# Retention plus MLP on one core: attention rewritten from whole-row scores per head to 128-token chunks with a running state

## The chip, the cores and the metric

The kernel runs on one core of one Trainium2 chip. The metric is device time in microseconds (us). "Span" is the profiled time from the first to the last instruction, about 2 us less than the time. PE is the tensor engine, PEld its weight loads, DVE the vector engine, ACT the scalar engine, POOL the GpSimd engine, SP the queue that issues DMAs. In a profile line, `L331` is a line of the kernel's source, and names such as `ml<-xt,win` are output tile and input tiles, with buffer numbers left out.

## The reference

Eight batches, eight heads, 576 tokens, head size 64. Retention is attention without a softmax, with a decay per head; its output is a 4,608 x 512 matrix that feeds an MLP of width 2,048.

```python
scores = (1/sqrt(64)) * q @ k.T
gamma  = 1 - 2.0 ** (-5 - head)
ret    = scores * where(i >= j, gamma ** (i - j), 0)
x      = (ret @ v), heads side by side          # 4608 x 512
h      = x @ w_in                               # 512 -> 2048
out    = (h * cos(h)) @ w_out                   # 2048 -> 512
```

`gamma ** (i - j)` splits into `gamma ** i * gamma ** -j`, so the decay can be put on rows and columns. Both kernels do that.

## The kernel before

It is scheduled by hand. For each batch, q and k come in 32-column pieces, are transposed 32 x 32 by DVE, and every head computes all scores of the lower triangle. ACT evicts them with the column decay, POOL masks the diagonal blocks, and PE multiplies with v.

```python
def attn_head_m1(self, b, c, hp):            # scores of one head
    for r in range(NCH):                     # five key blocks
        segs = [(0, 512), (512, wq - 512)] if r == 0 else [(0, wq)]
        ...
            te.matmul(dst, lhsT, rhs, ...)   # K = 64, N = 512,64,448,320,192,64
        ...
            act.activation(RT, PR, AF.Copy, scale=w_ap)      # eviction
        ...
        pool.affine_select(RTM, RT, ...)     # diagonal mask
# attn_head_m2: 12 matmuls v^T x scores into po_a and po_b
# batch loop: per head, m1 of the next head, then 4 units of MLP layer 1
#   (or 1 unit of layer 2), then m2 of this head
self.boot_pending = self.make_kv_issue_list(1) + [self.prologue_w_in, self.prologue_w_out]
# moe_mlp1_unit, first unit: waits until ALL MLP weights are in
self.S_w.wait(te, self.v_wout)
```

Of the kernel before, what the change touches and what calls it, by code (L numbers as in the profile page):

```python
# [6 lines left out]
ALU = mybir.AluOpType  # L8
# [4 lines left out]
B_, H_, S_, D_ = 8, 8, 576, 64  # L13
DFF = 2048
DM = H_ * D_
CH = 128
NCH = (S_ + CH - 1) // CH
TOK = B_ * S_
TB = 512
NTB = TOK // TB  # L20
QF = 4 * S_


class _Ctr:

    def __init__(self, handle, step=1):
        self.h = handle
        self.step = step
        self.count = 0

    def mark(self, inst):
        self.count += self.step
        inst.then_inc(self.h, self.step)
        return self.count

    def wait(self, eng, val):
        if val > 0:
            eng.wait_ge(self.h, val)


class _RR:

    def __init__(self, n):
        self.n = n
        self.next = 0
        self.last_consumer = [None] * n

    def take(self):
        s = self.next
        self.next = (self.next + 1) % self.n  # L50
        prev = self.last_consumer[s]
        return s, prev

    def set_consumer(self, s, key, val):
        self.last_consumer[s] = (key, val)


def bass_retnet_parallel__then__act_gcu_kernel(
    nc: bass.Bass,
    q: bass.AP,  # L60
    k: bass.AP,
    v: bass.AP,
    moe_w_in: bass.AP,
    moe_w_out: bass.AP,
    out: bass.AP,
):
    es = contextlib.ExitStack()
    with es:
        kern = _Kernel(nc, es, q, k, v, moe_w_in, moe_w_out, out)
        kern.build()  # L70


class _Kernel:
    def __init__(self, nc, es, q, k, v, w_in, w_out, out):
        self.nc = nc
        self.es = es
        self.q = q.tensor
        self.k = k.tensor
        self.v = v.tensor
        self.w_in = w_in.tensor  # L80
        self.w_out = w_out.tensor
        self.out = out.tensor

        self.gam = [float(1.0 - 2.0 ** (-5.0 - h)) for h in range(H_)]
        self.lng = [math.log(g) for g in self.gam]

        def sb(name, shape, dt):
            return nc.alloc_sbuf_tensor(name, shape, dt)

        self.XT = [sb(f"xt{c}", [128, TOK], BF16) for c in range(4)]  # L90
        self.WIN = sb("win", [128, 4 * DFF], BF16)
        self.WOUT = sb("wout", [128, 16 * DM], BF16)
        self.INQ = [sb(f"inq{i}", [128, QF], F32) for i in range(2)]
        self.INK = [sb(f"ink{i}", [128, QF], BF16) for i in range(2)]
        self.VNF = NCH * H_ * D_
        self.TQ = sb("tq32", [128, S_], F32)
        self.QH = [sb(f"qh{i}", [128, QF], BF16) for i in range(2)]
        self.KTB = [sb(f"ktb{i}", [128, QF], BF16) for i in range(2)]
        self.NVBF = 3
        self.VBF = [sb(f"vbf{i}", [128, self.VNF], BF16) for i in range(self.NVBF)]  # L100
        self.NRT = 12
        self.RT = [sb(f"rt{i}", [128, S_], BF16) for i in range(self.NRT)]
        self.NRM = 12
        self.RTM = [sb(f"rtm{i}", [128, CH], BF16) for i in range(self.NRM)]
        self.GT = sb("gt", [128, 16 * TB], BF16)
        self.NCB = 3
        self.CB = [sb(f"cb{i}", [128, TB], BF16) for i in range(self.NCB)]
        self.NOSB = 2
        self.OSB = [sb(f"osb{i}", [128, DM], F32) for i in range(self.NOSB)]
        self.IG = sb("ig", [128, S_], F32)  # L110
        self.IP = sb("ip", [128, 1], F32)
        self.UP = [sb(f"up{c}", [128, S_], F32) for c in range(4)]
        self.WV = sb("wv", [128, H_ * NCH], F32)
        self.C_LN8 = sb("c_ln8", [128, 1], F32)
        self.C_PIH = sb("c_pih", [128, 1], F32)

        self.PO_A = [nc.alloc_psum_tensor("po_a0", [128, 512], F32)]
        self.POB = nc.alloc_psum_tensor("po_b", [128, 512], F32)
        self.NPR = 6
        self.PR = [nc.alloc_psum_tensor(f"pr{i}", [128, 512], F32) for i in range(self.NPR)]  # L120

        def sem(name, step=1):
            return _Ctr(self.es.enter_context(nc.semaphore(name)), step)

        self.S_q = [sem("s_q0", 16), sem("s_q1", 16)]
        self.S_k = [sem("s_k0", 16), sem("s_k1", 16)]
        self.S_v = [sem(f"s_v{i}", 16) for i in range(3)]
        self.S_w = sem("s_w", 16)
        self.S_out = [sem("s_out0", 16), sem("s_out1", 16)]
        self.P = {  # L130
            "dve": sem("p_dve"),
            "act": sem("p_act"),
            "pool": sem("p_pool"),
            "pe": sem("p_pe"),
        }
        self.eng = {
            "dve": nc.vector,
            "act": nc.scalar,
            "pool": nc.gpsimd,
            "pe": nc.tensor,  # L140
            "sp": nc.sync,
        }

        self.pr_rr = _RR(self.NPR)
        self.rt_rr = _RR(self.NRT)
        self.rm_rr = _RR(self.NRM)
        self.cb_rr = _RR(self.NCB)
        self.osb_rr = _RR(self.NOSB)

        self.v_wout = 0  # L150
        self.v_win = 0
        self.seq_prep_last = {}
        self.seq_vcast = {}
        self.seq_pair_kt = {}
        self.seq_xt = {}
        self.seq_m1_last = {}
        self.seq_m2_last = {}
        self.seq_gt_last = {}
        self.seq_mlp2_last = {}
        self.n_out_dma = [0, 0]  # L160
        self.out_idx = 0
        self.seq_xtb_last = None
        self.seq_xtb = {}

    @staticmethod
    def sA(tile, fsize, p0, np_, c0, ncols, cstep=1):
        return bass.AP(tile, p0 * fsize + c0, [[fsize, np_], [cstep, ncols]])

    @staticmethod
    def sA3(tile, fsize, p0, np_, c0, n1, s1, n2, s2=1):  # L170
        return bass.AP(tile, p0 * fsize + c0, [[fsize, np_], [s1, n1], [s2, n2]])

    def mark(self, key, inst):
        return self.P[key].mark(inst)

    def wait(self, key_waiter, key_target, val):
        if val is not None and val > 0:
            self.P[key_target].wait(self.eng[key_waiter], val)

    def build(self):  # L180
        nc = self.nc
        blk = self.es.enter_context(nc.Block())

        @blk.tensor
        def _(eng):
            self.emit()

    def emit(self):
        self.prologue()
        self.issue_q_dmas(0)  # L190
        self.issue_kv_dmas(0, spread=False)
        self.issue_q_dmas(1)
        self.prep_wave(0)
        self.boot_pending = self.make_kv_issue_list(1) + [self.prologue_w_in, self.prologue_w_out]
        self.head_state = {}
        self.attn_head_m1(0, 0, 0)
        n_iter = B_ + 2
        for b in range(n_iter):
            has_att = b < B_
            j = b - 1  # L200
            has_moe = 0 <= j < NTB
            u1 = list(range(16)) if has_moe else []
            u2 = list(range(4)) if has_moe else []
            if has_att:
                self.pending_kv = self.make_kv_issue_list(b + 2) if b + 2 < B_ else []
                if b + 2 < B_:
                    self.issue_q_dmas(b + 2)
                heads = [(u // 2, u % 2) for u in range(8)]
                for u in range(8):
                    c, hp = heads[u]  # L210
                    if u < 7:
                        nc_, nhp = heads[u + 1]
                        self.attn_head_m1(b, nc_, nhp)
                    elif b + 1 < B_:
                        self.attn_head_m1(b + 1, 0, 0)
                    if u < 4:
                        for _ in range(4):
                            if u1:
                                self.moe_mlp1_unit(j, u1.pop(0))
                    else:  # L220
                        if u2:
                            self.moe_mlp2_unit(j, u2.pop(0))
                    if u == 3:
                        for dt in u1:
                            self.moe_mlp1_unit(j, dt)
                    self.attn_head_m2(b, c, hp)
                    if hp == 1:
                        self.xt_eval_A(b, c)
                    if u >= 4 and b + 1 < B_:
                        self.prep_pair(b + 1, u - 4)  # L230
# [451 lines left out]
```

## Time and profile before

| | before |
|---|---|
| time, median of 3 runs | 458.96 us |
| span | 457.0 us |
| first MLP matmul | 72.97 us |
| busy PE, ACT, DVE, POOL | 86, 56, 50, 38% |

The page of the kernel before: its span, the busy share of each engine, then PE and DMA in 40 equal slices of the span (tenths busy; one slice is 11.4 us).

```profile
span 457.0 us, 7084 instructions
...
PE 391.6 (86%) x2304; PEld 191.3 (42%) x2304; DVE 228.0 (50%) x372; ACT 257.5 (56%) x578; POOL 172.7 (38%) x409
...
PE   0283476999999999999999999999999999989987
...
DMA  9999999964696469746964696450011001101102
```

There are two stages. For six slices PE has little to do while DMA is full. After that PE is full. The waits of the kernel before (engine, tile and line, what it waited for: us in total, times, longest):

```profile
PE pr L418 <- DVE ktb L386: 20.3, 1, 20.3
...
PE po_a L495 <- POOL rtm L441: 14.3, 3, 9.0
...
PE pr L575 <- DMA wout<-in_moe_w_out_dram: 7.8, 1, 7.8
PE pr L575 <- ACT rt L428: 7.0, 27, 0.3
```

The first three are the start. The PE timeline of the kernel before (start us, length us, engine, line, operation, operands, count, idle before) shows the first MLP matmuls and, later, the steady repetition:

```profile
72.97 6.42 PE L575 MATMUL pr<-xt,win 128*128 128x512 bf16 x16 [7.76 <-DMA wout<-in_moe_w_out_dram]
...
144.43 3.63 PE L618 MATMUL pr<-wout,gt 128*128 128x512 bf16 x16 [0.26 <-ACT rt L428]
147.98 0.24 PE L495 MATMUL po_a<-rtm,vbf 128*64 128x128 bf16 x1
148.06 0.33 PE L521 MATMUL po_a<-rt,vbf 128*64 128x384 bf16 x1
...
148.92 0.97 PE L418 MATMUL pr<-qh,ktb 64*128 64x512 bf16 x6
150.15 1.04 PE L618 MATMUL pr<-wout,gt 128*128 128x512 bf16 x4 [0.26 <-ACT rt L428]
```

One head takes 150.15 - 144.43 = 5.72 us: 3.55 us of MLP (16 matmuls at about 0.216 us plus a short lead-in), 0.94 us of outputs, and 1.23 us of scores and a wait. Compare start times with start times: a record of an MLP matmul is about 379 ns long while the matmuls start 216 ns apart, so neighbouring records overlap.

### The profile page before, as it was taken

Reading aid. Unit: us, or ns where it says so; the run is one execution under the profiler, and the core shown is the slowest. Engines: PE = TensorE matmul, PEld = TensorE weight load, DVE = VectorE, ACT = ScalarE, POOL = GpSimd, SP = SyncE. Lnnn points to the kernel's source line nnn. Section 1 sums busy time; section 2 is a strip of 40 time slices with the busy share of each in tenths; the row PEclk is TensorE's granted clock in tenths of the full one; section 3 lists DMA queues with packets and bytes.
Section 4 is the critical chain, followed back from the end, with each engine's and each line's share of the span. In section 5 each row is a group of like instructions: output and inputs, shape, how many; then the busy total and the mean of one; then the engine's idle time right before and its main releaser. Section 6 shows DMA issues by size and latency. Waiting matters only on the chain.

```text
span 457.0 us, 7084 instructions
## 1 busy us (share of the span) xinstructions
PE 391.6 (86%) x2304; PEld 191.3 (42%) x2304; DVE 228.0 (50%) x372; ACT 257.5 (56%) x578; POOL 172.7 (38%) x409
## 2 busy tenths in 40 slices
PE   0283476999999999999999999999999999989987
PEld 0051232444444444444444444444444444434433
DVE  0440271546754675467546754675467542471641
ACT  8563272864686458645864586458645864260630
POOL 8093980445444544454445444532233222000000
PEclk9999999999999999999999999999999999999999
DMA  9999999964696469746964696450011001101102
GB/s 117 137 126 119 169 200 152 103 26 70 90 115 29 68 90 116 29 68 89 118 27 70 85 120 27 70 77 0 1 47 47 0 1 47 47 0 49 44 14 79
DMA packets 193908, 32.97 MB, mean 72 GB/s; under 512 B 186704, under 2 KB 188752, under 8 KB 193872
## 3 DMA queue, kind: packets, MB, share of 16 engines
q0 software_dynamic: 114448, 13.64, 48.4%
q1 hardware_dynamic: 79424, 18.88, 24.4%
q8 instruction: 19, 0.31, 0.3%
q14 instruction: 17, 0.14, 0.1%
HBM read 36.70 MB, written 9.44 MB: 101 GB/s over the span
## 4 chain that ended last, share of the span: by engine, by line
PE 75%; ACT 9%; DMA 8%; issue 4%; POOL 3%; DVE 0%; ACTq 0%; POOLq 0%; DVEq 0%
PE pr L575 29%; PE pr L618 28%; ACT rt L428 9%; PE pr L418 5%; PE po_a L495 5%; PE po_a L521 4%; DMA wout<-in_moe_w_out_dram 4%; DMA vbf<-in_v_dram 3%; PE po_b L507 2%; PE po_b L535 2%; POOL ink L329 1%; POOL vbf L339 1%; POOL rtm L441 0%; DVE gt L597 0%; ACT cb L587 0%
## 5 line engine op out<-in xcount | busy, mean ns | idle before, releaser
L428 ACT ACTIVATE rt<-pr,wv 128x512 bf16<-128x512 f32 (+5 forms) x384 | 148.6, 486 | 130.9 <-PE pr L418 130.9
L441 POOL TENSOR_SCALAR_AFFINE_SELECT rtm<-rt 128x128 bf16<-128x128 bf16 (+1 forms) x320 | 97.2, 324 | 198.3 <-ACT rt L428 191.9
L575 PE MATMUL pr<-xt,win 128*128 128x512 bf16 x576 | 132.3, 385 | 15.9 <-DMA wout<-in_moe_w_out_dram 7.8
L618 PE MATMUL pr<-wout,gt 128*128 128x512 bf16 x576 | 129.5, 379 | 10.2 <-ACT rt L428 7.0
L597 DVE TENSOR_TENSOR gt<-pr,cb 128x512 bf16<-128x512 f32 x144 | 97.1, 690 | 76.7 <-ACT cb L587 73.5
L587 ACT ACTIVATE cb<-pr,c_pih 128x512 bf16<-128x512 f32 x144 | 95.9, 688 | 48.6 <-PE pr L575 44.9
L575 PEld LDWEIGHTS pr<-xt,win 128*128 128x128 bf16 x576 | 54.7, 99 | 82.2 <-issue 12.8
L418 PE MATMUL pr<-qh,ktb 64*128 64x512 bf16 (+5 forms) x384 | 68.7, 301 | 20.3 <-DVE ktb L386 20.3
L618 PEld LDWEIGHTS pr<-wout,gt 128*128 128x128 bf16 x576 | 53.9, 98 | 75.0 <-ACT rt L428 9.9
L635 DVE COPY osb<-pr 128x512 f32<-128x512 f32 x36 | 24.9, 692 | 96.6 <-PE pr L618 96.6
L495 PE MATMUL po_a<-rtm,vbf 128*64 128x128 bf16 x256 | 54.5, 237 | 15.8 <-POOL rtm L441 14.3
L418 PEld LDWEIGHTS pr<-qh,ktb 64*128 64x128 bf16 (+1 forms) x384 | 29.2, 100 | 55.5 <-DVE ktb L386 20.3
L495 PEld LDWEIGHTS po_a<-rtm,vbf 128*64 128x64 bf16 x256 | 29.7, 116 | 44.7 <-issue 23.7
L521 PE MATMUL po_a<-rt,vbf 128*64 128x384 bf16 (+2 forms) x192 | 46.6, 291 | 0.0
L535 PE MATMUL po_b<-rt,vbf 128*64 128x64 bf16 x256 | 42.1, 201 | 0.0
L339 POOL DMA_DIRECT2D vbf<-in_v_dram x40 | 34.1, 858 | 10.6 <-issue 9.2
L329 POOL DMA_DIRECT2D ink<-in_k_dram x32 | 35.9, 1126 | 4.5 <-issue 4.5
L378 DVE STREAM_TRANSPOSE tq<-inq 128x576 f32<-128x576 f32 x32 | 24.9, 778 | 19.7 <-DMA ink<-in_k_dram 18.0
L546 DVE CAST xt<-po_b 64x64 bf16<-64x64 f32 x64 | 14.0, 219 | 31.5 <-PE po_b L507 31.1
L535 PEld LDWEIGHTS po_b<-rt,vbf 128*64 128x64 bf16 x256 | 28.9, 118 | 0.0
L380 DVE TENSOR_TENSOR qh<-tq,up 128x576 bf16<-128x576 f32 x32 | 24.2, 758 | 1.1
L386 DVE STREAM_TRANSPOSE ktb<-ink 128x576 bf16<-128x576 bf16 x32 | 24.7, 770 | 0.0
(19 smaller groups left out, 88.9 us busy)
## 6 DMA issues: line engine op xcount, KB each, us to landing
inq<-in_q_dram SPq DMA_DIRECT2D x32, 288.0 KB, 6.8
out_dram<-osb SPq DMA_DIRECT2D x36, 256.0 KB, 2.0
ink<-in_k_dram POOLq DMA_DIRECT2D x32, 144.0 KB, 6.1
vbf<-in_v_dram POOLq DMA_DIRECT2D x32, 128.0 KB, 4.7
win<-in_moe_w_in_dram POOLq DMA_DIRECT2D x8, 256.0 KB, 7.5
wout<-in_moe_w_out_dram POOLq DMA_DIRECT2D x1, 2048.0 KB, 20.0
vbf<-in_v_dram POOLq DMA_DIRECT2D x8, 64.0 KB, 2.6
```

Of the source, the lines that this page charges most:

```text
L329: self.S_k[slot].mark(pool.dma_start(dst, src))
L339: self.S_v[vpar].mark(pool.dma_start(dst, src))
L418: pm = self.mark("pe", te.matmul(dst, lhsT, rhs, start=True, stop=True))
L428: av = self.mark("act", act.activation(self.sA(self.RT[rts], S_, 0, ck, co, ncols), self.sA(self.PR[slot], 512, 0, ck, 0, ncols), AF.Copy, ...
L441: msk = pool.affine_select(self.sA(self.RTM[rms], CH, 0, ck, 0, ck), self.sA(self.RT[rts], S_, 0, ck, 0, ck), pattern=[[1, ck]], compare_o ...
L495: mm = te.matmul(self.sA(self.PO_A[0], 512, 64 * hp, 64, q0, ck), vmat, self.sA(self.RTM[rms], CH, 0, ck, 0, ck), start=(seen_a == 1), sto ...
L521: mm = te.matmul(self.sA(self.PO_A[0], 512, 64 * hp, 64, q0 + ck, nA), vmat, self.sA(self.RT[rts], S_, 0, ck, ck, nA), start=(seen_a == 1) ...
L535: mm = te.matmul(self.sA(self.POB, 512, 64 * hp, 64, 0, S_ - 512), vmat, self.sA(self.RT[rts], S_, 0, ck, 512 - q0, S_ - 512), start=(seen ...
L575: mm = te.matmul(self.sA(self.PR[slot], 512, 0, 128, 0, TB), self.sA(self.WIN, 4 * DFF, 0, 128, c2 * DFF + 128 * dt, 128), self.sA(self.XT ...
L587: sin = self.mark("act", act.activation(self.sA(self.CB[cb], TB, 0, 128, 0, TB), self.sA(self.PR[slot], 512, 0, 128, 0, TB), AF.Sin, bias= ...
L597: gm = self.mark("dve", ve.tensor_tensor(self.sA(self.GT, 16 * TB, 0, 128, dt * TB, TB), self.sA(self.PR[slot], 512, 0, 128, 0, TB), self. ...
L618: mm = te.matmul(self.sA(self.PR[slot], 512, 0, 128, 0, DM), self.sA(self.GT, 16 * TB, 0, 128, c3 * TB + 128 * stt, 128), self.sA(self.WOU ...
```

## The change

The intent is to do less attention work on PE and none that grows with the square of the sequence, to load q, k and v as they lie in memory, and to start the MLP sooner. Attention now goes in 40 chunks (eight batches of 128, 128, 128, 128 and 64 tokens), all eight heads at once. A chunk has four steps:

- T: eight PE transposes of q and k into PSUM bank `tp`, one ACT copy to `qk`.
- S: eight score matmuls, one DVE multiplication with a triangle, to `pt`.
- ST: four matmuls that add this chunk's k^T v to the state in PSUM bank `st`; DVE copies it masked to `sbd`.
- O: four matmuls from the old state and eight within the chunk, both into bank `tp` again; DVE scales to `xt`.

Steps are dealt out between the MLP's pieces, each of four 128x512 matmuls. The first layer of block j+1 alternates with the second layer of block j. A small recorder derives every wait from what each operation reads and writes. The diff, cut to its core (`...` marks what is left out; the comments are added here):

```diff
-    def prep_pair(self, b, c):                # DVE 32x32 transposes of q and k
-    def attn_head_m1(self, b, c, hp): ...     # ACT evictions, POOL masks
-    def attn_head_m2(self, b, c, hp): ...
+    def load_chunk(self, g):                  # fp32, rows of 64 values = 256 bytes
+        for i in (1, 0, 2):
+            self.P.add("sp", lambda e, i=i: e.dma_start(...))
+    def cast(self, g, engs): ...              # to bf16, v times its decay
+    def step_t(self, g): ...
+    def step_s(self, g): ...
+    def step_st(self, g): ...
+    def step_o(self, g): ...
+    def bank(self):
+        i = self.n_ml % 4
+        self.n_ml += 1
+        return i, self.ML[i]
+    def mlp1(self, j, f):
+        i, ps = self.bank()
...
+    def mlp2(self, j, t, qd):
+        if qd == 0:
+            self.m2 = self.bank()
...
+        if qd == 3:
+            self.P.add("act", lambda e: e.activation(self.OS[o].ap(), ps.ap(), AF.Copy), ...)
...
+        load_to(4)
+        cast_to(4, ("act", "dve", "pool"))
+        for s in range(4):
+            self.load_win(s)
+        for s in range(4):
+            self.load_wout(s)
+        load_to(self.NSTG)
+        done = need[0]
+        for g in range(done):                 # the first four chunks, alone
+            for st in steps(g):
+                st()
+        for j in range(-1, NTB):
...
+            for i in range(16):
+                if j + 1 < NTB:
+                    self.mlp1(j + 1, i)
+                while k < n * (2 * i + 1) / 32:
+                    todo[k]()
+                    k += 1
+                if j >= 0:
+                    self.mlp2(j, i // 4, i % 4)
+                while k < n * (2 * i + 2) / 32:
+                    todo[k]()
+                    k += 1
```

PSUM is laid out in eight banks of 512 fp32 columns: `tp` 1, `sc` (scores) 2, `st` 1, `ml` (both MLP layers) 4.

## The prediction

> **What bounds the kernel now.** The tensor engine (PE), in two ways. (a) Start: in the timeline PE has only batch 0's attention before 72.97 us, when the first MLP matmul starts; the waits name the `wout` load. The page's slices show DMA full for about 90 us. (b) From 73 us on PE is over 90% busy. The chain of waits repeats every 5.72 us, once per head: 16 MLP matmuls (3.55 us), 12 output matmuls (0.94), 6 score matmuls (0.97), and 0.26 waiting for ACT's score eviction. After the last head, two MLP blocks run alone at 0.216 us per 128x512 matmul (13.97 us for 64). DVE, ACT, POOL: 50, 56, 38%.
>
> **What changes.**
> - MLP: the same 1,152 matmuls x 0.216 = 249 us, the floor.
> - Attention on PE: 1,152 matmuls streaming 204,800 columns become 1,216 streaming about 141,000, transposes included. In the timeline the output matmuls of N=128 and 64 start 0.06 and 0.03 us apart, so weight loads hide. The Trainium skill, "TensorE: Matmul & The Clock Gate", section Back-to-back issue gap, gives 81 ns sustained for N=128; this trace shows about 60, which I use: 32 x 0.06 = 1.9 us for a full chunk, 1.1 for a 64-row chunk, 1.8 on average. Before: 8 heads x 2.2 = 17.4 us per batch; after: 5 x 1.8 = 9. Saved: about 8 us for each of 7 batches in the PE-bound stage.
> - New stalls: one PSUM bank (`tp`) serves transposes and outputs; each chunk is a chain (transpose, ACT copy of 1,024, scores, DVE mask of 1,024, output, DVE scaling). Extrapolating the traced evictions (ACT 310 ns at 64 to 687 at 512 columns, DVE 690 at 512), copy and mask take 1.1 and 1.2 us. With 1 or 2 MLP pieces of 0.86 us between steps, copy and scaling are sometimes late: 0.5 us a chunk, 15 us.
> - DVE loses 64 transposes; ACT loses 149 us of score evictions, gains about 40 of copies; POOL loses 320 masks, gains 3 casts a chunk (about 2.5 us). All stay under 65%.
> - Start: loads come in 256-byte pieces, and MLP weights are asked for after four chunks (about 22 us) instead of at 48.7. Before, they took 24 us from issue. I expect the first MLP matmul near 30 us, the first MLP block with five chunks until about 57 (partly starved by the chunk chain), no later weight stall.
>
> **Sum.** 57 + remaining MLP 235 + 31 chunks x 1.8 = 55 + stalls 15 + tail 4 = 366 us span, plus 2 us between span and time: 368 us, range 350 to 400. All of it is on the critical path, since PE is it. Faster by over 2%: 0.98; within 2%: 0.015; slower: 0.005.
>
> **What would show each step.** First `win` matmul at 25 to 38 us; `wout` waits under 5 us. In the middle, one MLP block (128 matmuls) plus about 4.4 chunks takes 37 to 40 us. Attention matmuls start about 0.06 us apart. PE waits on ACT (`qk`) and DVE (`xt`) total 10 to 30 us. POOL under 40%, DVE 50 to 60%. No gap between the last block's two layers.
>
> **What would make it wrong.** Loads of 128 weight columns not hiding behind N=128 matmuls (100 ns each: +35 us). The `tp` chain stalling 1 us a chunk more (+35). 256-byte pieces still delaying `wout` past 70 us (+15). Score pairs on disjoint rows, and output pairs on disjoint columns, running together (-15).

## The result, and the profile after

| | before | after |
|---|---|---|
| time, median of 4 runs | 458.88 us | 390.91 us |
| span | 457.0 us | 389.2 us |
| first MLP matmul | 72.97 us | 38.02 us |
| from there to the end | 384.0 us | 351.2 us |
| busy PE, ACT, DVE, POOL | 86, 56, 50, 38% | 84, 42, 48, 23% |

The ratio is 0.8531 (95% interval 0.8512 to 0.8549). A ratio is the mean time of one kernel's fast runs over that of the other's of the same rounds, so it is not quite the ratio of the medians quoted.

The change is faster, inside the predicted range, but 23 us slower than the predicted 368. Of the gain, 35 us come from the earlier start of the MLP and 33 us from the time after it. The page of the changed kernel (a slice is 9.7 us here):

```profile
span 389.2 us, 5828 instructions
...
PE 326.4 (84%) x2325; PEld 160.0 (41%) x2368; DVE 185.4 (48%) x283; ACT 162.3 (42%) x231; POOL 91.3 (23%) x128
...
PE   1156877889988999989889999998999899989996
...
PEclk9999989999999999999999999999999999999999
```

PE is the engine with most to do again, but its digits are not an unbroken row of nines. `PEclk` is the granted clock in tenths; the 8 in its sixth slice comes up again below. The waits of the changed kernel that concern PE:

```profile
PE sc L247 <- ACT qk L236: 16.7, 14, 9.8
PE ml L331 <- ACT os L361: 15.3, 25, 0.9
PE tp L227 <- DVE xt L309: 6.5, 7, 2.0
...
PE ml L331 <- DVE xt L309: 3.9, 3, 1.9
...
PE ml L331 <- DVE gt L340: 3.5, 4, 1.0
```

The second line, first-layer matmuls that wait for the copy of a second-layer output, is nowhere in the prediction. The PE timeline of the changed kernel at the start:

```profile
7.31 0.60 PE L227 MATMUL tp<-idn,nat 128*128 128x128 bf16 x4 [2.15 <-ACT nat L210]
17.72 0.61 PE L247 MATMUL sc<-qk 64*128 64x128 bf16 x8 [9.80 <-ACT qk L236]
...
38.02 1.48 PE L331 MATMUL ml<-xt,win 128*128 128x512 bf16 x3 [1.20 <-DVE xt L309]
...
72.77 1.04 PE L331 MATMUL ml<-xt,win 128*128 128x512 bf16 x4 [1.88 <-DVE xt L309]
```

And ACT's timeline just before those first scores:

```profile
16.12 0.63 ACT L210 ACTIVATE nat<-stg 128x512 bf16<-128x512 f32 x1 [2.99 <-DMA stg<-in_q_dram]
16.66 1.00 ACT L236 ACTIVATE qk<-tp 128x1024 bf16<-128x1024 bf16 x1
```

Chunk 0's transposes are finished before 8 us, but ACT copies them at 16.66 us, because the casts of q for all four first chunks stand ahead of the copy in ACT's order, and the fourth has to arrive first. Then four chunks run one after another, 5.5 us each. The first MLP block (first layer of block 0 with five chunks) lasts from 38.02 to 72.77 us, 34.8 us.

In the middle, the PE timeline of the changed kernel shows what the steps cost and the new wait:

```profile
196.44 0.61 PE L227 MATMUL tp<-idn,nat 128*128 128x128 bf16 x8
196.88 1.03 PE L351 MATMUL ml<-wout,gt 128*128 128x512 bf16 x4
198.71 1.04 PE L331 MATMUL ml<-xt,win 128*128 128x512 bf16 x4 [0.80 <-ACT os L361]
199.68 0.40 PE L247 MATMUL sc<-qk 64*128 64x128 bf16 x8
200.01 1.04 PE L351 MATMUL ml<-wout,gt 128*128 128x512 bf16 x4
200.88 1.03 PE L331 MATMUL ml<-xt,win 128*128 128x512 bf16 x4
201.74 0.39 PE L267 MATMUL st<-nat 128*128 128x128 bf16 x4
201.97 1.03 PE L351 MATMUL ml<-wout,gt 128*128 128x512 bf16 x4
```

Two MLP pieces with nothing between start 0.864 us apart (200.01 to 200.88 is one). With S between they start 1.30 us apart (198.71 to 200.01), so S costs 0.44 us. ST costs 200.88 to 201.97 less 0.864, or 0.23; T and O come out in the same way at 0.45 and 0.67. A full chunk takes 1.78 us of PE, 56 ns for each of its 32 matmuls on average: what the prediction had (1.9).

From 196.88 to 198.71 is 1.83 us, though: more than a full piece is lost. The blocks in the middle take (341.19 - 72.77) / 7 = 38.3 us (341.19 us is where the last pair of layers starts).

### The profile page after: what moved, and what is told of

Same layout as the page of the kernel before. It is cut to its first block, busy times and chain, and to the rows that moved or that the text cites. A ratio compares the mean times of both kernels' runs of the same rounds, so it can differ in the third digit from the quotient of the medians.

```text
span 389.2 us, 5828 instructions
## 1 busy us (share of the span) xinstructions
PE 326.4 (84%) x2325; PEld 160.0 (41%) x2368; DVE 185.4 (48%) x283; ACT 162.3 (42%) x231; POOL 91.3 (23%) x128
## 4 chain that ended last, share of the span: by engine, by line
PE 73%; ACT 12%; DVE 7%; issue 3%; SPq 3%; DMA 1%; DVEq 0%; ACTq 0%
PE ml L331 31%; PE ml L351 30%; ACT qk L236 5%; ACT os L361 4%; PE tp L227 4%; PE sc L247 3%; ACT cb L338 3%; DVE gt L340 3%; PE tp L299 3%; SPq L185 3%; DVE pt L255 2%; DVE xt L309 2%; PE st L267 1%; DMA stg<-in_q_dram 1%; PE tp L289 1%
## 5 line engine op out<-in xcount | busy, mean ns | idle before, releaser
L340 DVE TENSOR_TENSOR gt<-ml,cb 128x512 bf16<-128x512 f32 x144 | 99.5, 691 | 160.3 <-ACT cb L338 142.1
L338 ACT ACTIVATE cb<-ml,cpi 128x512 bf16<-128x512 f32 x144 | 98.9, 687 | 168.8 <-PE ml L331 168.8
L331 PE MATMUL ml<-xt,win 128*128 128x512 bf16 x549 | 147.4, 387 | 24.9 <-ACT os L361 15.3
L351 PE MATMUL ml<-wout,gt 128*128 128x512 bf16 x560 | 143.4, 380 | 2.2 <-issue 0.9
L331 PEld LDWEIGHTS ml<-xt,win 128*128 128x128 bf16 x576 | 50.4, 99 | 84.0 <-ACT os L361 22.9
L351 PEld LDWEIGHTS ml<-wout,gt 128*128 128x128 bf16 x576 | 52.2, 98 | 57.2 <-ACT os L361 1.2
L212 POOL CAST nat<-stg 128x512 bf16<-128x512 f32 (+1 forms) x72 | 42.5, 613 | 140.6 <-PE st L267 117.1
L214 POOL TENSOR_TENSOR nat<-stg,wv 128x512 bf16<-128x512 f32 (+1 forms) x40 | 41.7, 1043 | 61.8 <-PE tp L299 38.6
L255 DVE TENSOR_TENSOR pt<-sc,tri 128x1024 bf16<-128x1024 f32 (+1 forms) x40 | 44.3, 1109 | 13.8 <-PE sc L247 13.7
L236 ACT ACTIVATE qk<-tp 128x1024 bf16<-128x1024 bf16 (+1 forms) x40 | 37.3, 933 | 24.1 <-PE tp L227 24.1
L247 PE MATMUL sc<-qk 64*128 64x128 bf16 (+1 forms) x320 | 16.4, 226 | 16.7 <-ACT qk L236 16.7
L247 PEld LDWEIGHTS sc<-qk 64*128 64x128 bf16 (+1 forms) x320 | 9.5, 102 | 33.8 <-ACT qk L236 26.1
L276 DVE TENSOR_TENSOR sbd<-st,bdm 128x512 bf16<-128x512 f32 x32 | 21.8, 681 | 0.0
L299 PE MATMUL tp<-pt,nat 128*64 128x128 bf16 (+1 forms) x320 | 16.7, 230 | 2.9 <-DVE pt L255 2.9
```

Source lines behind the costliest of these rows:

```text
L212: fn = lambda e, dst=dst, src=src: e.tensor_copy(dst, src)
L214: self.P.add(engs[2], lambda e: e.tensor_tensor(ap(nat, 3 * DM, 0, n, 2 * DM, [D, H], [1, D]), ap(stg, 3 * DM, 0, n, 2 * DM, [D, H], [1, D ...
L236: self.P.add("act", lambda e: e.activation(ap(qk, 1024, 0, 128, 0, [128, 8], [1, n]), tb.rearrange("p (c n) -> p c n", c=8)[:, :, 0:n], AF ...
L247: inst = e.matmul(ap(self.SC, 1024, 0, n, hp * 512 + c * 128, [1, n]), ap(qk, 1024, 64 * hp, 64, c * 128, [1, n]), ap(qk, 1024, 64 * hp, 6 ...
L255: self.P.add("dve", lambda e: e.tensor_tensor(ap(pt, 1024, 0, n, 0, [128, 8], [1, n]), ap(self.SC, 1024, 0, n, 0, [128, 8], [1, n]), ap(se ...
L299: inst = e.matmul(ap(self.T, 512, 64 * hp, 64, c * 128, [1, n]), ap(na, 3 * DM, 0, n, 2 * DM + (2 * c + hp) * D, [1, D]), ap(pt, 1024, 0, ...
```

## The experiments

Twelve kernels ran, all with correct results, each timed in three rounds against the kernel before. "Against the change" is (ratio - 0.8531) x 457.9 us. The 95% interval of a ratio reaches 0.6 to 1.3 us to each side (2.7 for e9_jit_bank), so a difference of under about 1.5 us between two rows is not clear of noise.

| run | what | median us | ratio | against the change |
|---|---|---|---|---|
| e1_jit | first casts in order of need | 384.74 | 0.8397 | -6.1 |
| e2_bank | MLP banks 2 + 2 | 369.10 | 0.8071 | -21.1 |
| e8_onebank | MLP banks 2 + 1 | 373.48 | 0.8164 | -16.8 |
| e3_split | banks 2 + 1, own bank for O | 366.07 | 0.7993 | -24.6 |
| e4_wlate | w_out loads later | 392.72 | 0.8565 | +1.6 |
| e5_unp | head halves not alternating | 391.77 | 0.8573 | +1.9 |
| e9_jit_bank | e1 + e2 | 366.30 | 0.7966 | -25.9, two speeds (below) |
| e6_jit_split | e1 + e3 | 364.80 | 0.7974 | -25.5 |
| e11_jit_bank_wl | e1 + e2 + e4 | 362.14 | 0.7900 | -28.9 |
| e10_all | e1 + e3 + e4 | 358.46 | 0.7827 | -32.2 |
| e12_serial | steps not interleaved | 495.95 | 1.0826 | +105 |
| e7_before_early | kernel before, weights earlier | 466.52 | 1.0195 | - |

### The late start: order on ACT (e1_jit)

```diff
-        cast_to(4, ("act", "dve", "pool"))
+        cast_to(1, first)
...
         for g in range(done):
-            for st in steps(g):
-                st()
+            self.step_t(g)
+            if g + 1 < done:
+                cast_to(g + 2, first)
+            self.step_s(g)
+            self.step_st(g)
+            self.step_o(g)
```

> The casts of the first four chunks are moved to one chunk ahead of their use, so ACT's first copy of transposes no longer stands behind the cast of the fourth chunk's q. Theory 'order on ACT' (the start is late because of the order in ACT's queue): the 9.8 us wait of the first scores shrinks to under 2 us, the first MLP matmul moves from 38.0 to 28 to 31 us, and the whole gets 5 to 9 us shorter than 390.9 (382 to 386). Rival 'loads bind the start' (bandwidth decides when the first MLP block can end): the first MLP matmul moves, but the block's end near 72.8 us does not, and the whole gains under 2 us.

The wait of the scores in this run, and its PE timeline:

```profile
PE sc L247 <- ACT qk L236: 7.6, 13, 1.1
```

```profile
29.32 1.48 PE L331 MATMUL ml<-xt,win 128*128 128x512 bf16 x3 [1.19 <-DVE xt L309]
...
64.97 1.21 PE L331 MATMUL ml<-xt,win 128*128 128x512 bf16 x4 [1.88 <-DVE xt L309]
```

The longest wait of scores fell from 9.8 to 1.1 us. The first MLP matmul came 8.7 us sooner, the end of the first block 7.8 us sooner, the whole 6.1 us sooner. The order of the casts was the cause of that part of the late start; the edit moves those on DVE and POOL too, and that ACT's order was the one that held up the scores is read from the trace (the copy at 16.66 us directly behind the cast at 16.12). The 1.7 us lost again after the first block go with the clock: between 65.7 and 69.1 us it was granted at 0.50 in this run and not in the changed kernel, and 3.4 us at half speed are worth 1.7. The one run of the four without that stretch, by its mean clock of 0.996, took 383.34 us. The rival, that bandwidth fixes the block's end, fell for this kernel.

### The wait for the output copy: PSUM rotation (e2_bank)

Four banks are handed out in turn. For each 128-token output the program takes one bank for a first-layer unit, one for the second-layer output, then three for first-layer units. The next taking is the fourth after the second-layer output's, so with four banks it gets the same bank, and it comes immediately after that output's last matmul. It must wait for ACT's copy (0.60 us) each time.

```diff
-    def bank(self):
-        i = self.n_ml % 4
+    def bank1(self, j):
+        i = self.n_ml % (4 if j == 0 else 2)
         self.n_ml += 1
         return i, self.ML[i]
+    def bank2(self):
+        self.n_m2 += 1
+        i = 2 + self.n_m2 % 2
+        return i, self.ML[i]
```

> First MLP layer gets PSUM banks 0 and 1 (all four in the block without a second layer), second layer gets 2 and 3, instead of four in one rotation. Theory 'bank collision' (every fifth taking of a bank lands on the one whose output copy has just started): the waits of first-layer matmuls on the output copy fall from 15.3 us to under 2, the middle blocks from 38.3 to about 36.5 us, the whole by 12 to 17 us to 374 to 379. Rival 'the wait only hides another' (ACT or DVE would be late anyway): under 5 us gained, with the wait turning up on gt or cb.

The only waits of first-layer matmuls (line 336 here) that the list of this run still has, and then, from its PE timeline, where the second block starts and where the last pair of layers starts:

```profile
PE ml L336 <- DVE xt L309: 5.2, 5, 1.9
...
PE ml L336 <- issue: 1.6, 9, 0.3
```

```profile
72.76 1.04 PE L336 MATMUL ml<-xt,win 128*128 128x512 bf16 x4 [1.87 <-DVE xt L309]
...
322.69 1.03 PE L336 MATMUL ml<-xt,win 128*128 128x512 bf16 x4
```

For comparison, the last pair of layers in the changed kernel, its start and one collision:

```profile
341.19 1.02 PE L331 MATMUL ml<-xt,win 128*128 128x512 bf16 x4 [0.78 <-DVE gt L340]
...
347.23 1.03 PE L351 MATMUL ml<-wout,gt 128*128 128x512 bf16 x4
348.95 1.04 PE L331 MATMUL ml<-xt,win 128*128 128x512 bf16 x4 [0.69 <-ACT os L361]
```

In e2_bank the wait on `os` is gone, and so is the one on `gt`. A middle block takes (322.69 - 72.76) / 7 = 35.7 us, 2.6 less. I expected 12 to 17 us and got 21: the idle time listed (15.3 us, 0.69 us for one wait in the undisturbed last pair of layers) starts only at the modelled end of the last matmul, while the starts there are 1.72 us apart (347.23 to 348.95) instead of 0.864, so one collision costs 0.86 us. The mean clock was the same in both runs (0.995 and 0.996). This wait is by itself nearly the difference between the measured 391 us and the predicted 368; but the agreement is partly luck, since two other terms were off in opposite directions (below).

### One bank for transposes and outputs (e3_split and e8_onebank)

```diff
+        self.TO = nc.alloc_psum_tensor("to", [128, 512], F32)
...
-        self.ML = [nc.alloc_psum_tensor(f"ml{i}", [128, 512], F32) for i in range(4)]
+        self.ML = [nc.alloc_psum_tensor(f"ml{i}", [128, 512], F32) for i in range(3)]
...
-                    ap(self.T, 512, 0, 128, c * 128, [1, n]),
+                    ap(self.TO, 512, 0, 128, c * 128, [1, n]),
...
+    def bank1(self, j):
+        i = self.n_ml % (3 if j == 0 else 2)
...
+    def bank2(self):
+        return 2, self.ML[2]
```

The lines with `TO` are in e3_split only. The second layer always has bank 2, the first layer banks 0 and 1.

> Second layer gets one bank of its own, first layer two, and the bank this frees takes the attention outputs, so that transposes and outputs no longer share one. Theory 'shared transpose bank': as with the bank split alone, plus the waits of transposes on the xt scaling (6.5 us, most of it before 73 us) and part of the starved first block go: 4 to 8 us better than the bank split alone, 367 to 373. Rival 'the single second-layer bank brings the copy wait back': no better than the bank split alone, with waits of second-layer matmuls on the output copy.

> Only the bank part of the third run: one bank for the second layer, two for the first, transposes and outputs sharing a bank as in the changed kernel (a PSUM bank stays unused). Splits the 24.8 us of that run: if the single bank costs 2 to 3 us against two, 371 to 373 us, and the separate output bank was worth about 6; if the single bank is free, 369, and the output bank was worth 3.

One bank for the second layer instead of two costs 4.3 us (0.8164 against 0.8071). The separate output bank is then worth 7.8 us (0.7993 against 0.8164). Both are more than I had estimated, and they partly cancel: e3_split is only 3.6 us better than e2_bank, just under the 4 to 8 expected, because its rival was in part right (second-layer matmuls wait 3.0 us for `os` again). The end of the first block in e3_split:

```profile
65.35 1.04 PE L335 MATMUL ml<-xt,win 128*128 128x512 bf16 x4 [1.88 <-DVE xt L310]
```

It comes at 65.35 us instead of 72.77, and no wait of transposes on `xt` is left. So the shared bank did cost what the prediction had feared of it, but in the first block and not in the middle: between 72.8 and 341 us the changed kernel's transposes wait 0.5 us for `xt` in total.

### Loads (e4_wlate, e6_jit_split, e9_jit_bank, e10_all, e11_jit_bank_wl)

```diff
-        for s in range(4):
-            self.load_wout(s)
...
             def prep():
+                if 4 <= g < 8:
+                    self.load_wout(g - 4)
```

> The four loads of the second layer's weights are asked for later, one each ahead of the transposes of chunks 4 to 7, so that input chunks 5 to 8 compete with less. Theory 'loads bind the first block': input loads after 22 us land sooner, the first block (38.0 to 72.8 us) shortens by 2 to 6 us, the whole with it. Rival 'the chunk chain binds the first block': within 1 us of 390.9, or slower if the weights now come late.

Alone it gained nothing. POOL's cast of chunk 6's v starts at 41.21 us instead of 46.23, so the loads did come sooner, but the first block still ended at 73.11 us: the chain of steps bound it (the waits of transposes on `xt` are 6.5 us as before). The 1.6 us more go with the clock again: it was 0.50 from 73.4 to 76.7 us, and the one run with a mean clock of 0.996 took 390.92 us, as long as the changed kernel.

> Early casts and the two-and-two bank split together. If the late start and the bank collision are independent (one ends before 73 us, the other begins after it), the gains of 6.2 and 21.8 us add up: 362 to 364 us. If one hides the other, 366 or more.

Its four runs lie between 361.02 and 367.3 us. The times go with the mean clock: 361.02 at 0.995, 366.3 to 367.3 at 0.981 to 0.986, and the profiled one has a clock of 0.50 from 43.7 to 47.0, 50.5 to 57.2 and 71.0 to 74.3 us. At about the clock of the changed kernel (0.996) the gains add up: 29.9 us together against 7.6 and 21.8 for the fastest run of e1_jit and the middle of e2_bank. But only one run says so.

> Early casts, one bank for the second layer and a bank of its own for the attention outputs. With the start shortened by both, the first MLP matmul comes at 26 to 28 us and the first block ends near 57 us, as the prediction had it; the whole is 358 to 361 us, if the loads keep up. Rival 'loads now bind the start': the first block ends at 60 us or later, with waits of transposes on the casts, and the whole is 362 or more.

The rival was right here: the first MLP matmul came at 26.36 us, but the first block ended at 64.07, only 1.3 us before that of e3_split. A new wait of PE in this run shows why:

```profile
PE st L268 <- POOL nat L215: 4.6, 1, 4.6
```

Chunk 6's state matmuls wait for POOL's cast of its v, and the cast for the load, which shares the DMA engines with the MLP weights. The wait ends at 46.86 us, and from 44.7 to 51.4 us the clock was granted at 0.50, so the matmuls after it ran slowly as well. The two remedies that had each gained little here belong together:

> Early casts, one bank for the second layer, a bank of its own for the attention outputs, and the second layer's weights asked for later. Theory 'loads bind the start once the chain is short': the 4.6 us wait of chunk 6's state matmuls on its v goes, the first block ends at 58 to 61 us instead of 64.1, and the whole falls from 364.8 to 358 to 362, although the later weight loads alone gained nothing. Rival 'the chain still binds': 364 to 366.

> Early casts, the two-and-two bank split (transposes and outputs share a bank, as in the changed kernel), and the later weight loads. If loads were what ate the gain of the early casts here (366.3 against an expected 362 to 364, with a 3.6 us wait of chunk 6's state on its v), 360 to 364; if the shared bank's chain binds, 365 to 367.

In e10_all the 4.6 us wait is gone, and the PE timeline reads

```profile
58.35 1.04 PE L335 MATMUL ml<-xt,win 128*128 128x512 bf16 x4 [1.88 <-DVE xt L310]
```

so the first block now ends 14.4 us sooner than in the changed kernel. At 358.46 us (ratio 0.7827, interval 0.7802 to 0.7852) it beats both kernels. Its clock is 1.00 from 33.4 us to the end, so part of its gain over e6_jit_split is clock. With transposes and outputs sharing a bank, e11_jit_bank_wl stays at 362.14, inside the 360 to 364 expected if the loads were what ate the gain.

### Do pairs of small matmuls run together? (e5_unp)

```diff
-            for c in range(4):
-                for hp in range(2):
+            for hp in range(2):
+                for c in range(4):
```

> Scores and within-chunk outputs are issued all four of one head half first, then four of the other, instead of alternating. Theory 'pairs run together' (neighbours on disjoint rows, or disjoint columns, of the array overlap): eight scores take 0.44 to 0.46 us instead of 0.33, eight outputs about 0.45 instead of 0.35, so about 0.2 us a chunk and 6 to 9 us in all: 397 to 400 us. Rival 'the spacing of 41 ns has nothing to do with pairs': within 1.5 us of 390.9 and the same spacings.

The PE timeline of this run, to be set beside the same stretch above:

```profile
199.29 1.04 PE L331 MATMUL ml<-xt,win 128*128 128x512 bf16 x4 [0.78 <-ACT os L361]
200.26 0.41 PE L247 MATMUL sc<-qk 64*128 64x128 bf16 x8
200.60 1.04 PE L351 MATMUL ml<-wout,gt 128*128 128x512 bf16 x4
```

From 199.29 to 200.60 is 1.31 us, and it was 1.30 with alternating halves. The 0.33 us that I had read as 41 ns for a score was a misreading, since it leaves out a gap before the first score. Counted from MLP piece to MLP piece, a score costs 54 to 56 ns either way, and order makes at most 1.9 us of difference.

This does not mean that pairs do not overlap. In the changed kernel's timeline above, eight transposes fill 0.61 us and four state matmuls 0.39, but eight scores only 0.40: they start in the time of four. The single starts in the packed trace say the same: two scores 3 to 4 ns apart, the next two 55 to 67 ns later. In this run the two are 13 to 14 ns apart and the next two come just as late. So pairs ran together in both orders, and this experiment did not separate them as I had meant it to. What they save is lost at the edges: the first score starts 0.31 us after the last MLP matmul instead of 0.216, and the next MLP matmul 0.15 us after the last pair instead of 0.056. The cause of these two gaps of 0.1 us was not tested.

### What interleaving is worth (e12_serial)

```diff
-            n, k = len(todo), 0
+            for st in todo:
+                st()
+            n = k = 0
```

> The changed kernel with one thing undone: in each block all chunks' steps come before the block's MLP matmuls instead of between them. Theory 'interleaving hides the chunk chain' (a chunk takes 5.5 us alone, 1.8 of it PE): 36 chunks lose about 3.7 us each, up to 130 us in all, less the first block's part, which is starved already: 480 to 520 us, slower than the kernel before. Rival 'the chain overlaps from chunk to chunk anyway': under 30 us lost.

The granted clock in 40 slices (a line of the page; tenths of full speed), and the three longest waits of PE in this run:

```profile
PEclk9999998599957996699659995999569966999999
```

```profile
PE sc L247 <- ACT qk L236: 50.5, 40, 10.0
PE tp L227 <- DVE xt L309: 24.9, 32, 0.9
PE tp L299 <- DVE pt L255: 21.0, 39, 0.8
```

Without interleaving the same arithmetic is 8% slower than the kernel before. The three waits of the chain grow from 26.1 us (16.7, 6.5 and 2.9) to 96.4. Beside that the granted clock was lower, 0.80 to 0.83 in the middle windows against 1.00. How much of the remaining 35 of the 105 us it took I did not separate.

### Was the start of the kernel before only a matter of asking late? (e7_before_early)

```diff
-self.boot_pending = self.make_kv_issue_list(1) + [self.prologue_w_in, self.prologue_w_out]
+self.boot_pending = [self.prologue_w_in, self.prologue_w_out] + self.make_kv_issue_list(1)
```

> The kernel before, with one thing changed: the MLP weights are asked for ahead of batch 1's k and v instead of behind them. Theory 'order of loads' (the late first MLP matmul is only a matter of asking late): first MLP matmul at 55 to 64 us instead of 73, and 8 to 16 us gained (442 to 450). Rival 'bandwidth' (the loads that come before the first MLP matmul fill the DMA engines whatever their order): within 4 us of 458, with batch 1's first scores now waiting for k.

Neither theory. It got 1.95% slower (interval 1.77 to 2.14%, so against a line of 2% the verdict is unclear), and the first MLP matmul moved from 72.97 to 81.65 us. A wait of PE, and one of POOL in the first 85 us:

```profile
PE po_a L495 <- POOL rtm L441: 31.1, 4, 15.9
```

```profile
POOL ink L329 <- issue: 14.1, 2, 13.6
```

PE waits for masks, because POOL, which makes them, stands for up to 13.6 us in front of its own DMA issues and waits for nothing else that the profile shows, while the DMA engines are full. The waits for masks grew by 16.8 us (from 14.3), and the wait of 7.8 us for `w_out` went: together 9.0, about what the first MLP matmul lost. Whether the queue is short of room or something else holds these issues is open. What the run does show is that the early start is not to be had in the old kernel by asking for weights sooner. In the changed kernel the first MLP matmul needs only four chunks and a quarter of `w_in` (it waited for `xt`, not for `win`), and its eight weight loads were issued by POOL in 6.2 us without standing still; which of these the early start rests on was not tested apart. Nor was the kernel before run with its first MLP unit waiting for `w_in` alone: up to the 7.8 us of its wait for `w_out` might have been had that way.

## Why the prediction was right, and where it was off

- **Direction and range: right.** PE was and is the bound, and the two sources named, an earlier start and less attention on PE, gave 35 and 33 us. That split is read from the two timelines; no run undoes one source alone.
- **PE cost of a chunk: right.** 1.78 us measured for a full chunk, 1.9 predicted; 56 ns a matmul on average, and weight loads of 128 columns do hide. The Trainium skill, "TensorE: Matmul & The Clock Gate", section Back-to-back issue gap, gives 81 ns sustained for N=128; the trace gives 56, which is that section's isolated figure.
- **"First MLP matmul near 30 us": off by 8.** It came at 38.02, because ACT's in-order queue put chunk 0's copy behind the fourth chunk's cast. Shown by e1_jit (29.32). That order stood in the program and could have been read.
- **"First MLP block until about 57": off by 16 in all.** The block itself took 34.8 us instead of 27. The shared `tp` bank was 7.4 us of the 16 (e3_split: 2.6 before the first MLP matmul, 4.8 in the block). Moreover the first MLP matmuls run at half speed there. The Trainium skill, "TensorE: Matmul & The Clock Gate", Part 1 (the clock gate), describes a cold array with 427 ns for N=512. The trace agrees: a piece of four takes about 1.7 us near 41 us and 0.864 later (and the first 16 MLP matmuls of the kernel before took 6.42 us, against 3.63 later). The clock line shows nines there only because the packed trace has no clock record before 45.22 us. From then on the matmuls start 216 ns apart, but the clock was back at 0.50 from 52.04 to 55.46 us (the 8 in the clock line), after a wait of 1.98 us for `xt`; e3_split has no such stretch, and 1.7 of its 4.8 us can be that. The prediction left all this out. With the casts, the banks and the loads mended, e10_all ends the first block at 58.35 us, near the 57.
- **"Stalls 15" in the middle: the term that failed.** The suspected stalls were there for only 5.4 us between 72.8 and 341 us (waits on `qk` 1.9, on `xt` 0.5 and 2.7, on `pt` 0.3). A stall that I did not see, the PSUM rotation, cost 21 us (e2_bank). Without it the time from the first block's end to the end of the span is 367.3 - 72.8 = 294.5 us, against 309 predicted; with it 316.4.
- **"A middle block takes 37 to 40 us": confirmed at 38.3, for the wrong reason.** It is 35.7 us plus 2.6 us of collisions. A total that matches does not confirm its terms.
- **"Waits on `qk` and `xt` total 10 to 30 us": 27.1 us, but 23.8 us of that came before 75 us.** POOL at 23% was right; DVE at 48% lay just under the range; the load of `w_out` was never waited for; the last pair of layers followed each other with no gap but the same bank wait of 0.69 us.
- **Listed risks:** slow weight loads did not occur. Pairs did run together, but gained nothing, since about 0.1 us is lost before and after each row of them (trace, section on e5_unp). Loads became the limit only after the chain was shortened (e6_jit_split against e10_all).

## What to carry to other kernels

When several producers take buffers from one rotation, write down which buffer each taking meets: a ring that is sound on average can meet the most recently filled one every time, and separate rings over the same four banks cost nothing here. In a program with in-order engines, read each engine's order for the first use of each result, above all at the start, where one operation that waits for a late load holds up everything behind it. Test remedies in combination as well: the later loads of `w_out` were worth nothing alone and 6.7 us (0.7974 to 0.7827, the better clock included) once the chain in front of them had been shortened. And before you explain a difference of a few us between two runs, compare their granted clock stretch by stretch: here one stretch of 3.4 us at half speed was worth 1.7 us.

## What the Trainium skill lacked or had wrong

- "TensorE: Matmul & The Clock Gate", section Back-to-back issue gap, states a sustained spacing of about 131 ns for N=512 with its weight loads, and 81 ns for N=128. These runs show 216 ns (13.97 us for 64, in which the last record's 0.38 us is counted whole) and 56 ns; the isolated formula on the same page, N/2.4 + 2.5 ns, fits both.
- The same page, Part 3 (Packing small matmuls), says in its list of what overlaps that weight loads overlap matmuls in flight only where the row group differs, though its paragraph on the mechanism also names a background weight buffer. In the MLP all loads use all 128 rows, a load's record is 98 ns long, and matmuls still start 216 ns apart, so they do overlap.
- The same Part says that matmuls on disjoint 32-row tiles run together. The trace agrees for 64-row halves writing to two PSUM banks: pairs start 3 to 4 ns apart. No page gives a figure for the gaps at the edges of such a row, about 0.1 us before and after it here, with which eight scores (0.44 us) cost as much as eight transposes (0.45).
- The same page, Part 4 (PE-mode transpose), gives about 275 to 390 ns for a 128x128 transpose, as the time of one, and no spacing. Here a record of one is 233 ns long on average, and in a row of eight they start 56 ns apart (0.45 us for the row).
- No page that I read gives the cost of reusing a PSUM bank straight after its last matmul with a copy in between. Here it was 0.86 us each time for 128x512 fp32 (the copy itself 0.60 us).
